# Second layer's first product in seven block products instead of eight, with block operands kept in DRAM

## The chip, the cores and the metric

The kernel runs on one core of one Trainium2 chip. The metric is device time in microseconds (us) of one execution. Engines are called PE (TensorE, the matmuls), PEld (its weight loads, which run beside it), DVE (VectorE), ACT (ScalarE), POOL (GpSimd) and SP (SyncE, which here issues the DMAs).

## The reference

An attention stage gives 2176 tokens of 512 features (4 batches of 512 tokens and 32 state rows); a first layer (512 to 1024 and back, with a softmax and a layer norm between) transforms them; a second layer follows, and it is the one that changes:

```python
def _moe2_ref(x, w_in, w_out) -> np.ndarray:      # 2176 x 512, 512 x 2048, 2048 x 512
    h = x @ w_in
    sp = np.where(h > 20.0, h, np.log1p(np.exp(np.minimum(h, 20.0))))
    g = h * np.tanh(sp)                            # the Mish function
    return (g @ w_out).astype(np.float32)
```

The weights come in as 64-bit floats and are narrowed to 32 bits in the kernel.

## The kernel before, in words

Tokens are 17 tiles of 128. Each product is computed in a split form: an operand is cut in a high part (a cast on ACT) and a low part (the subtraction of the cast, on DVE), and three matmuls stand for one, low by high, high by high and high by low. A matmul's width is the number of tokens or features that stream through it.

Phase 1 holds attention, the first layer, and what the second needs first. The order of its steps is written out in a string, PLAN, with flags that say which engine takes a step; among them `lw`, `lo`, `lx` load w_in, w_out and x; `wi` narrows w_in into w_in_t; `sp` multiplies the states by w_in_t; `a0` to `a3`, `c`, `e` run the first layer of a tile, and `d` its last product (pm, L470), whose result x goes to SBUF. `early_w2` prepares the first weights of layer 2. The program builder then sets a static order for every engine.

Phase 2 (from L559) is the second layer. The 2048 hidden features are 16 blocks f of 128. The tokens go in blocks of 3, 3, 4, 4 and 3 tiles; the first two blocks run side by side through all f, the others one after the other. `load_w2(f)` loads 512 KB of w_in and of w_out each, narrows them (`narrow`: two scalings on ACT or DVE, L45 to L50, and two DVE steps, L52 and L54), casts the high part (L134) and subtracts (L135); from then on the weights stay in SBUF. `stage_h` multiplies x by the weights of one f: twelve matmuls (four slices of 128 features, three each) of 384 or 512 columns into a bank hp of a ring of two (L590). Mish reads hp twice on ACT (L596 for the high part gh, L597 for a_), and DVE subtracts for the low part gl (L598). `stage_o`, three f behind, adds gh and gl times the output weights to po, one of six banks for each tile, three matmuls of 512 columns per tile and f (L610 to L612). For later blocks the split of x (L579, L580) is made at f = 0. A tile whose po is done is copied on ACT (L622) and stored.

## Time and profile before

| | us |
|---|---|
| three runs | 619.14, 620.29, 623.5 |
| median | 620.29 |
| profiled execution, its own time | 618.53 |
| its span, first to last instruction | 616.8 |
| PE busy in the span | 588.1 |
| DVE, ACT, POOL busy | 297.2, 266.3, 35.3 |

The profile page gives busy time per engine, a line of 40 slices of the span (tenths busy), the DMA queues, the chain of work that ended last, and the costliest groups of instructions. The trace behind it gives the start of each instruction. A busy PE is not a PE at its peak: matmuls overlap, one begins before the last has drained, so what one adds to the time is the distance from its start to the next one's.

### The profile page before, as it was taken

How to read it: one execution, taken by the hardware profiler on the slowest of the kernel's cores; microseconds unless marked ns; L12 is line 12 of the kernel's file. 1: busy time of each engine (PE TensorE's matmuls, PEld its weight loads, DVE VectorE, ACT ScalarE, POOL GpSimd, SP SyncE). 2: the span in 40 equal slices, each digit the busy share in tenths (PEclk: the TensorE clock that was granted, in tenths of full speed). 3: DMA queues.
4: the chain of work that ended last, by engine and by line, in shares of the span. 5: the costliest groups of instructions: out<-in, count | busy, mean ns of one | idle time of the engine just before them, and what ended most of it. 6: DMA issues, size and time to landing. Idle time of an engine off the chain costs nothing.

```text
span 616.8 us, 7791 instructions
## 1 busy us (share of the span) xinstructions
PE 588.1 (95%) x3048; PEld 499.5 (81%) x3048; DVE 297.2 (48%) x476; ACT 266.3 (43%) x485; POOL 35.3 (6%) x107
## 2 busy tenths in 40 slices
PE   5379999999999999999999999999999999999997
PEld 3227598779799999898998988888888888898896
DVE  3999998898578676688731121111221111211110
ACT  3786767566477652455732224221223211332211
POOL 0002131103122100000000000000000000000000
PEclk9999999999999999999999999999999999999999
DMA  8913524433445582364500002000001000011001
GB/s 346 412 42 102 156 70 123 169 103 118 172 137 175 176 223 77 137 201 137 175 1 0 1 0 104 0 1 0 1 0 70 1 0 1 0 37 33 1 1 51
DMA packets 26916, 54.77 MB, mean 89 GB/s; under 512 B 3072, under 2 KB 12800, under 8 KB 26368
## 3 DMA queue, kind: packets, MB, share of 16 engines
q1 hardware_dynamic: 26880, 54.28, 26.3%
q8 instruction: 24, 0.39, 0.3%
q14 instruction: 12, 0.10, 0.0%
HBM read 41.95 MB, written 12.32 MB: 88 GB/s over the span
## 4 chain that ended last, share of the span: by engine, by line
PE 81%; DMA 9%; DVE 5%; SPq 2%; ACT 2%; issue 1%; POOL 0%; DVEq 0%; ACTq 0%
PE hp L590 29%; PE pm L470 11%; PE po L612 10%; PE po L611 10%; PE po L610 10%; PE ph L372 6%; PE sr L301 2%; DMA wo<-in_w_out 2%; DMA w<-in_w2i 1%; DMA xT_t<-in_xT 1%; DMA wi<-in_w_in 1%; PE ph L378 1%; DMA w<-in_w2o 1%; SPq L447 1%; DMA td<-tt 1%; DVE gw_lo L354 1%
## 5 line engine op out<-in xcount | busy, mean ns | idle before, releaser
L596 ACT ACTIVATE gh<-hp 128x384 fp32r<-128x384 f32 (+1 forms) x80 | 42.6, 533 | 215.2 <-PE hp L590 206.4
L590 PE MATMUL hp<-x_lo,w2ih 128*128 128x384 f32 (+1 forms) x320 | 114.9, 359 | 1.0 <-ACT a__2378 L597 1.0
L590 PE MATMUL hp<-x_hi,w2il 128*128 128x384 f32 (+1 forms) x320 | 114.6, 359 | 0.0
L590 PE MATMUL hp<-x_hi,w2ih 128*128 128x384 f32 (+1 forms) x320 | 114.5, 358 | 0.0
L612 PE MATMUL po<-w2oh,gl 128*128 128x512 f32 x272 | 107.0, 393 | 0.0
L611 PE MATMUL po<-w2oh,gh 128*128 128x512 f32 x272 | 106.8, 393 | 0.0
L610 PE MATMUL po<-w2ol,gh 128*128 128x512 f32 x272 | 106.5, 391 | 0.0
L470 PE MATMUL pm<-ln_lo,gw_hi 128*128 128x256 f32 (+1 forms) x256 | 75.5, 296 | 0.3 <-ACT e L266 0.2
L470 PE MATMUL pm<-ln_hi,gw_hi 128*128 128x256 f32 (+1 forms) x256 | 74.5, 291 | 0.0
L470 PE MATMUL pm<-ln_hi,gw_lo 128*128 128x256 f32 (+1 forms) x256 | 74.3, 290 | 0.0
L590 PEld LDWEIGHTS hp<-x_lo,w2ih 128*128 128x128 f32 x320 | 60.1, 188 | 8.6 <-ACT a__2378 L597 1.3
L590 PEld LDWEIGHTS hp<-x_hi,w2ih 128*128 128x128 f32 x320 | 60.1, 188 | 7.3
L590 PEld LDWEIGHTS hp<-x_hi,w2il 128*128 128x128 f32 x320 | 60.1, 188 | 5.4
L612 PEld LDWEIGHTS po<-w2oh,gl 128*128 128x128 f32 x272 | 51.0, 188 | 11.3
L610 PEld LDWEIGHTS po<-w2ol,gh 128*128 128x128 f32 x272 | 51.1, 188 | 10.1 <-DVE raw_d L484 0.4
L611 PEld LDWEIGHTS po<-w2oh,gh 128*128 128x128 f32 x272 | 51.0, 188 | 9.8
L470 PEld LDWEIGHTS pm<-ln_lo,gw_hi 128*128 128x128 f32 x256 | 48.2, 189 | 1.7 <-DVE x_lo L478 0.5
L470 PEld LDWEIGHTS pm<-ln_hi,gw_hi 128*128 128x128 f32 x256 | 48.3, 189 | 0.7 <-issue 0.5
L470 PEld LDWEIGHTS pm<-ln_hi,gw_lo 128*128 128x128 f32 x256 | 48.4, 189 | 0.2
L49 ACT ACTIVATE w<-w 128x512 uint32<-128x512 uint32 x28 | 19.1, 683 | 17.4 <-DMA w<-in_w2o 8.9
L372 PE MATMUL ph<-swh,aThi 128*128 128x512 f32 x64 | 21.5, 417 | 4.5 <-DVE swl L330 4.5
L52 DVE SCALAR_TENSOR_TENSOR w<-w 128x512 uint32<-128x512 uint32 x32 | 21.9, 689 | 6.4 <-ACT w L49 6.3
(283 smaller groups left out, 755.9 us busy)
## 6 DMA issues: line engine op xcount, KB each, us to landing
w<-in_w2i SPq DMA_DIRECT2D x16, 512.0 KB, 4.1
w<-in_w2o SPq DMA_DIRECT2D x16, 512.0 KB, 3.9
td<-tt SPq DMA_DIRECT2D x13, 512.0 KB, 2.9
...
wo<-in_w_out SPq DMA_DIRECT2D x4, 1024.0 KB, 10.7
...
wi<-in_w_in SPq DMA_DIRECT2D x8, 512.0 KB, 8.0
...
```

Of the source, the lines that this page charges most:

```text
L49: nc.scalar.activation(out=low, in_=low, func=AF.Copy, scale=TOP_BITS)
L52: nc.vector.scalar_tensor_tensor(out=low, in0=high, scalar=3, in1=low, op0=ALU.logical_shift_left, op1=ALU.bitwise_or)
L301: nc.tensor.matmul(out=sr[:, j, :], lhsT=x_[:, k, :], rhs=a2[:, r0 // NS:r0 // NS + 2, k, :], start=k == 0, stop=k == 3)
L354: nc.vector.scalar_tensor_tensor(out=gw_lo[sl], in0=wr[:, k, :], scalar=g_k, in1=f32(gw_hi[sl]), op0=ALU.mult, op1=ALU.subtract)
L372: nc.tensor.matmul(out=ph[:, hf * 512:(hf + 1) * 512], lhsT=a_[:, c * P:(c + 1) * P], rhs=w_[:, q, hf * 512:(hf + 1) * 512], start=n == 0, ...
L378: nc.tensor.matmul(out=ph[:, hf * 512:(hf + 1) * 512], lhsT=xs[:, p, :], rhs=w_in_t[:, p, hf * 512:(hf + 1) * 512], start=p == 0, stop=p == 3)
L470: nc.tensor.matmul(out=pm[:, :n], lhsT=w_[:, k, m * P:(m + 1) * P], rhs=l_[:, c0:c0 + 4 * len(blk), k, :], start=cnt == 0, stop=cnt == 23)
L590: nc.tensor.matmul(out=hp[:, :n], lhsT=w_[:, k * P:(k + 1) * P], rhs=x_[:, k, x0:x0 + n], start=cnt == 0, stop=cnt == 11)
L596: nc.scalar.activation(out=gh, in_=hp[:, :n], func=AF.Mish)
L610: nc.tensor.matmul(out=po[bi, j], lhsT=gh[:, c], rhs=wl, start=f == 0, stop=False)
L611: nc.tensor.matmul(out=po[bi, j], lhsT=gh[:, c], rhs=wh, start=False, stop=False)
L612: end = nc.tensor.matmul(out=po[bi, j], lhsT=gl[:, c], rhs=wh, start=False, stop=f == NF - 1)
```

## The change

The first product of layer 2, h = x · w_in, is computed by blocks. For a pair of f's (a group, fp, eight of them) the weights are cut into four blocks (two halves of the 512 input features, two f's), the tokens of a pass into two halves, and the four block results come from seven products of sums of blocks (Winograd's form of Strassen's algorithm) rather than eight of the blocks themselves. Passes are of 6, 6 and 5 tiles, so a half has 384, 384 or 320 columns, and a product is six matmuls (`product`, L727). Of the three results that several outputs share, one is copied from PSUM by ACT (L763); seven DVE additions (L748) combine the products; Mish then reads SBUF (L757, L758).

The seven weight operands of a group, high and low, are made in pass 0 (`pieces_in`: two loads, narrowing at L46 to L55, four additions L165 to L168, five casts L175 and five subtractions L176), written to DRAM (L179), and fetched back in passes 1 and 2 (`fetch_in`, L210), into a ring of two slots. The first three groups' are made in phase 1. The seven operands of x are sums (`x_sums`, L234 to L237) and splits (`x_split`, L247 and L248); for pass 0 they are made in phase 1 after the last tiles, for a later pass in the last group of the one before. The out products (L708 to L710) are as many as before, cut in four parts that stand between the products of the next group. PLAN and its flags are new throughout.

```diff
-@N=01010011001111100 @O=0001 @P=11111111111111111 @Q=110111010011110010111001 @R=01000011 @S=11111111
-@V=00011110 @W=0001111111101100 @X=10000011 @Y=00001111111111111 @Z=00011011110110101
-lo,1,1 lb,0 lx,0 gn,1,1 sa,0 lw,1,1 ts,0 lw,2,0 fs,0,0 wi,1,1 lw,1,0 lw,3,0 te,0 tn,0 rs,0,0 lw,2,1 lw,0,1
-wi,3,0 wi,0,0 wi,1,0 fs,0,1 lw,3,1 lg sp,0,0,0,0 lo,1,0 sp,0,0,1,0 lo,0,0 tt,0,0 rs,0,1 wi,2,1 sp,0,0,0,1
...
-w,0 w,1 d,4,1 a1,15 e,10 a0,16 d,4,0 a2,14 c,13 d,5,0 a1,16 w,2 d,5,1 a2,16 a3,14 e,13 e,12 a2,15 a3,15 c,15
-d,6,1 a3,16 c,16 c,14 e,15 w,4 e,14 d,6,0 e,16 d,7,1 d,7,0 w,3
...
+a3,4 a1,6 c,3 a1,7 s2,0 lx,3 e,2 c,4 e,4 a3,5 a0,9 a0,8 a1,9 a2,6 a2,7 a3,6 a3,7 c,6 c,5 ln,2 e,3 a1,8
...
-    def load_w2(f, pool):
-        for nm, src in (("i", w2i[f]), ("o", w2o[f])):
-            hi = pool.tile([P, 512], F32R, name=f"w2{nm}h{f}")
-            lo = pool.tile([P, 512], F32R, name=f"w2{nm}l{f}")
-            w64 = w64_p.tile([P, 512, 2], U32, tag="w64", name="w64")
-            nc.sync.dma_start(out=w64, in_=src)
-            w = f32(w64[..., 0])
-            narrow(nc, w, w64, eng('W', f, False, True), how(12 + f))
+
+
+    A11, A12, A22, S1, S2, S3, S4 = range(7)
+    B11, B21, B22, T1, T2, T3, T4 = range(7)
...
+    def ring(fp):
+
+        if fp % 2 == 0:
+            return [[(0, 7, sw_o.tile([P, 7, 256], F32R, tag=t, name="w2" + t))] for t in ("swh", "swl")]
+        t = x2p.tile([P, 2, 6, 256], F32R, tag="x1", name="w2r")
+        r = wx_p.tile([P, 2, 1, 256], F32R, tag="wx1", name="w2r1")
...
+    def pieces_in(fp, stage=False):
+
+        w = []
+        for j in range(2):
...
+        s1, s2, s3, s4 = ea[:, :256], ea[:, 256:], eb[:, :256], eb[:, 256:]
+        on = eng('G', fp, nc.vector, nc.gpsimd)
+        on.tensor_tensor(out=s1, in0=a21, in1=a22, op=ALU.add)
+        on.tensor_tensor(out=s3, in0=a11, in1=a21, op=ALU.subtract)
...
+        for i, n, src in ((A11, 1, a11), (A12, 1, a12), (A22, 1, a22), (S1, 2, ea), (S3, 2, eb)):
+            if i in (A11, S1):
+                yield
+            src = src.rearrange("p (n c) -> p n c", c=256)
+            hi, lo = (operands(place, i, n) for place in places)
...
+            nc.vector.tensor_tensor(out=lo, in0=src, in1=f32(hi), op=ALU.subtract)
+        for place, d in zip(places, kept[fp]):
+            for i, n, w in place:
+                nc.sync.dma_start(out=d[:, i:i + n], in_=f32(w))
+        if stage:
+            staged.add(fp)
+        else:
+            W["i", fp] = places
...
+    def pieces_out(fp, pool=None):
+        for j in range(2):
+            f = 2 * fp + j
+            if pool is None:
...
+            w, _ = load64(w2o[f], 1, f)
+            yield
...
-            eng('L', f, nc.gpsimd, nc.vector).tensor_tensor(out=lo, in0=w, in1=f32(hi), op=ALU.subtract)
-            W[nm, f] = (hi, lo)
+            eng('H', fp, nc.vector, nc.gpsimd).tensor_tensor(out=lo, in0=w, in1=f32(hi), op=ALU.subtract)
...
+    def fetch_in(fp):
+        W["i", fp] = ring(fp)
+        for place, d in zip(W["i", fp], kept[fp]):
+            for i, n, w in place:
+                nc.sync.dma_start(out=f32(w), in_=d[:, i:i + n])
...
+
+    HALVES = [([("a", 0, 384)], [("a", 384, 384)]),
+              ([("c", 0, 256), ("d", 0, 128)], [("c", 256, 256), ("d", 128, 128)]),
+              ([("d", 256, 320)], [("d", 576, 320)])]
+    xop = {}
...
+    def x_sums(ps):
+
+        t = x2p.tile([P, 4, 2, 384], F32, tag="x1" if ps == 0 else "x0", name="xsum")
+        for o, n, b11, b21, b12, b22 in halves(ps):
+            t1, t2, t3, t4 = (t[:, i, :, o:o + n] for i in range(4))
+            nc.vector.tensor_tensor(out=t1, in0=b12, in1=b11, op=ALU.subtract)
+            nc.vector.tensor_tensor(out=t2, in0=b22, in1=t1, op=ALU.subtract)
+            nc.vector.tensor_tensor(out=t3, in0=b22, in1=b12, op=ALU.subtract)
+            nc.vector.tensor_tensor(out=t4, in0=b21, in1=t2, op=ALU.subtract)
...
+    def x_split(ps, i):
+        x = tl["E"].tile([P, 2, 2, 384], F32R, tag=f"xo{i}", name=f"xo{i}")
+        for o, n, b11, b21, b12, b22 in halves(ps):
...
+            nc.scalar.copy(out=hi, in_=src)
+            nc.vector.tensor_tensor(out=lo, in0=src, in1=f32(hi), op=ALU.subtract)
+        xop[i] = (x[:, 0], x[:, 1])
...
-                if d0 < 6:
-                    o = slice(d0 * P, d0 * P + n)
-                    nc.scalar.copy(out=x_hi[:, m, o], in_=pm[:, :n])
-                    nc.vector.tensor_tensor(out=x_lo[:, m, o], in0=pm[:, :n], in1=f32(x_hi[:, m, o]), op=ALU.subtract)
-                elif d0 < 10:
-                    o0 = (d0 - 6) * P
-                    copy(out=raw_c[:, m, o0:o0 + n], in_=pm[:, :n])
-                else:
-                    o0 = (d0 - 10) * P
-                    copy(out=last_view()[:, m, o0:o0 + n], in_=pm[:, :n])
+                o0 = (d0 - base) * P
+                copy(out=raw[t][:, m, o0:o0 + n], in_=pm[:, :n])
...
-        def stage_h(bi, f, n):
...
-            if bi == 0 and f >= NE:
-                load_w2(f, w2p)
-            hp = ps_g.tile([P, 512], F32, tag="hp", name="hp")
-            wh, wl = W["i", f]
-            cnt = 0
-            for k in range(4):
-                for w_, x_ in ((wh, x_lo), (wh, x_hi), (wl, x_hi)):
-                    nc.tensor.matmul(out=hp[:, :n], lhsT=w_[:, k * P:(k + 1) * P], rhs=x_[:, k, x0:x0 + n],
-                                     start=cnt == 0, stop=cnt == 11)
...
-            gs[bi, f] = (gh, gl)
-
         po = {}
...
-        seq = [(bi, f) for f in range(NF) for bi in range(2)] + [(bi, f) for bi in range(2, 5) for f in range(NF)]
-        for i in range(len(seq) + LAG - 2):
-            if i < len(seq):
-                bi, f = seq[i]
-                stage_h(bi, f, sizes[bi] * P)
...
+        def out_parts(ps, fp):
+
+            n, nh = tiles[ps], tiles[ps] // 2
+            f0, f1 = 2 * fp, 2 * fp + 1
+            if fp < NFP - 1:
+                low, high = range(nh), range(nh, n)
+                parts = [[(f0, j) for j in low], [(f1, j) for j in low],
+                         [(f1, j) for j in high], [(f0, j) for j in high]]
...
+                m = -(-len(steps) // 4)
...
+            def product(*terms):
+                r = bank()
+                cnt = 0
+                for a, x in terms:
+                    wh, wl = (operands(place, a) for place in W["i", fp])
+                    for k in range(2):
+                        for w_, x_ in ((wh, x[1]), (wh, x[0]), (wl, x[0])):
+                            nc.tensor.matmul(out=r, lhsT=w_[:, 0, k * P:(k + 1) * P], rhs=x_[:, k, :n],
+                                             start=cnt == 0, stop=cnt == 6 * len(terms) - 1)
+                            cnt += 1
+                return r
+
+            def step(a, b):
...
+                if last:
+                    x_split(ps + 1, b)
+                for _ in range(1 if b in (B11, T3) else 2):
+                    next(more, None)
+                return r
...
+            def bank():
+                return ps_g.tile([P, 512], F32, tag="hp", name="hp")[:, :n]
...
+            part = iter(parts)
+            m1_ = temp("m1")
+            nc.scalar.copy(out=m1_, in_=step(A11, B11))
+            active(add("c0", m1_, step(A12, B21)), 0, 0)
+            next(part)()
+            u2 = add("u2", m1_, step(S2, T2))
+            u3 = add("u3", u2, step(S3, T3))
+            next(part)()
+            active(add("c1", u3, step(A22, T4)), 1, 0)
+            m5 = step(S1, T1)
+            active(add("c2", u3, m5), 1, 1)
+            u4 = add("m1", u2, m5)
+            next(part)()
+            active(add("c0", u4, step(S4, B22)), 0, 1)
+            next(part)()
...
+        for ps in range(NPASS):
+            for fp in range(NFP):
+                ahead = fp + 1
+                more = iter(())
+                if ps == 0 and 2 <= ahead < NFP:
+                    more = pieces_out(ahead, w2p)
+                    if ahead in staged:
+                        fetch_in(ahead)
+                    else:
+                        more = chain(pieces_in(ahead), more)
+                elif ps > 0 and ahead < NFP:
+                    fetch_in(ahead)
+                if ps + 1 < NPASS and fp == NFP - 1:
+                    fetch_in(0)
+                if ps + 1 < NPASS and fp == NFP - 2:
+                    x_sums(ps + 1)
+                group(ps, fp, parts, more)
+                for _ in more:
```

On PE, in the middle of phase 2 of before, one run of `stage_h` and the out products ahead of it read (name, operation, operands, width; a wait names the engine that must have got that far; DMAHW5 and the like are DMA queues):

```order
L611 MATMUL po<-w2oh_3204,gh 128x512
L612 MATMUL po<-w2oh_3204,gl 128x512
L590 MATMUL hp<-x_lo,w2ih_3346 128x384 [waits Activation_49]
L590 MATMUL hp<-x_hi,w2ih_3346 128x384
L590 MATMUL hp<-x_hi,w2il_3347 128x384
L590 MATMUL hp<-x_lo,w2ih_3346 128x384
L590 MATMUL hp<-x_hi,w2ih_3346 128x384
L590 MATMUL hp<-x_hi,w2il_3347 128x384
L590 MATMUL hp<-x_lo,w2ih_3346 128x384
L590 MATMUL hp<-x_hi,w2ih_3346 128x384
```

After, in the second pass, out products lead to the fifth, sixth and seventh product of a group (xo_3595, xo_3613, xo_3642 are three of the operands of x, w2swh and w2swl the ring's weights):

```order
L727 MATMUL hp<-xo_3595,w2swl 128x384
L727 MATMUL hp<-xo_3613,w2swh 128x384 [waits DVE_49]
L727 MATMUL hp<-xo_3613,w2swh 128x384
L727 MATMUL hp<-xo_3613,w2swl 128x384
L727 MATMUL hp<-xo_3613,w2swh 128x384 x2
L727 MATMUL hp<-xo_3613,w2swl 128x384
L727 MATMUL hp<-xo_3642,w2swh 128x384 [waits DVE_49]
L727 MATMUL hp<-xo_3642,w2swh 128x384
L727 MATMUL hp<-xo_3642,w2swl 128x384
L727 MATMUL hp<-xo_3642,w2swh 128x384 x2
L727 MATMUL hp<-xo_3642,w2swl 128x384
L708 MATMUL po<-w2ol_2516,gh 128x512 [waits Activation_49]
```

Where one run of twelve waited once, for ACT, three runs of six now follow each other, each with a wait for DVE, without out products between them.

On DVE, in the stretch in which layer 2's weights are prepared, before (w_2816 and so on are loaded weights, w2il and w2ol low parts):

```order
L54 SCALAR_TENSOR_TENSOR w_2816<-w_2816 128x512 [waits DVE_49]
L598 TENSOR_TENSOR gl<-a__2515,gh 128x384 [waits PE_49,Activation_49]
L135 TENSOR_TENSOR w2il_2815<-w_2816,w2ih_2814 128x512 [waits Activation_49]
L45 TENSOR_SCALAR w_2826<-w_2826 128x512 [waits DMAHW5_49]
L52 SCALAR_TENSOR_TENSOR w_2826<-w_2826 128x512 [waits DVE_49,Activation_49]
L45 TENSOR_SCALAR w_2892<-w_2892 128x512 [waits DMAHW6_49]
L54 SCALAR_TENSOR_TENSOR w_2826<-w_2826 128x512 [waits DVE_49]
L52 SCALAR_TENSOR_TENSOR w_2892<-w_2892 128x512 [waits DVE_49,Activation_49]
L598 TENSOR_TENSOR gl<-a__2543,gh 128x384 [waits PE_49,Activation_49]
L45 TENSOR_SCALAR w_2902<-w_2902 128x512 [waits DMAHW7_49]
L54 SCALAR_TENSOR_TENSOR w_2892<-w_2892 128x512 [waits DVE_49]
L135 TENSOR_TENSOR w2ol_2825<-w_2826,w2oh_2824 128x512 [waits Activation_49]
```

After, in a group of pass 0 (c, u and m are the results of the additions of hp):

```order
L53 SCALAR_TENSOR_TENSOR w_2831<-w_2831 128x512 [waits DMAHW0_49,Activation_49]
L55 SCALAR_TENSOR_TENSOR w_2831<-w_2831 128x512 [waits DVE_49]
L748 TENSOR_TENSOR u_2733<-hp,u_2714 128x384 [waits PE_49]
L165 TENSOR_TENSOR w_2817<-w_2831 128x256 [waits DVE_49]
L166 TENSOR_TENSOR w_2831<-w_2817,w_2831 128x256
L167 TENSOR_TENSOR w_2817<-w_2817 128x256 [waits DVE_49]
L168 TENSOR_TENSOR w_2831<-w_2817 128x256 [waits DVE_49]
L53 SCALAR_TENSOR_TENSOR w_2879<-w_2879 128x512 [waits DMAHW2_49,Activation_49]
L748 TENSOR_TENSOR c_2753<-hp,u_2733 128x384 [waits PE_49]
L55 SCALAR_TENSOR_TENSOR w_2879<-w_2879 128x512 [waits DVE_49]
L748 TENSOR_TENSOR c_2766<-hp,u_2733 128x384 [waits PE_49]
L748 TENSOR_TENSOR m_2772<-hp,u_2714 128x384
```

Between the narrowing steps of the loaded weights there now stand the additions that read hp and wait for PE, and those of the weights among each other; two narrowing steps in a row wait one for the other.

On SP, which issues the DMAs in order, before, in the same stretch:

```order
L131 DMA w_2664<-in_w2i 128x1024 [waits DMAHW5_49,DVE_49]
L131 DMA w_2674<-in_w2o 128x1024 [waits DMAHW6_49,DMAHW1_49,DVE_49]
L131 DMA w_2740<-in_w2i 128x1024 [waits DMAHW7_49,DMAHW2_49,DVE_49]
L131 DMA w_2750<-in_w2o 128x1024 [waits DMAHW3_49,DMAHW0_49,DVE_49]
L131 DMA w_2816<-in_w2i 128x1024 [waits DMAHW4_49,DMAHW1_49,DVE_49]
L131 DMA w_2826<-in_w2o 128x1024 [waits DMAHW2_49,DVE_49]
```

After (k4h and k4l are the DRAM copies of a group's operands):

```order
L151 DMA w_2898<-in_w2o 128x1024 [waits DMAHW3_49,DMAHW2_49,DVE_49]
L179 DMA k4h<-w2swh 128x1792 [waits DMAHW4_49,Activation_49]
L151 DMA w_2988<-in_w2i 128x1024 [waits DMAHW6_49,DVE_49]
L179 DMA k4l<-w2swl 128x1792 [waits DVE_49]
L151 DMA w_3002<-in_w2i 128x1024 [waits DMAHW7_49,DMAHW0_49]
L151 DMA w_3052<-in_w2o 128x1024 [waits DMAHW3_49,DVE_49]
L179 DMA k5h<-w2r_3013 128x256 [waits DMAHW1_49,Activation_49]
L179 DMA k5l<-w2r_3013 128x256 [waits DVE_49]
L151 DMA w_3071<-in_w2o 128x1024 [waits DMAHW0_49,DVE_49]
```

The loads alternated, each behind the load three before it; now the stores of one group's operands, which wait for the last cast and the last subtraction, stand ahead of the next group's loads.

## Rows read from the trace of the kernel before

**Rows 1.** The page, busy us, share of the span, and count by engine.

```profile
PE 588.1 (95%) x3048; PEld 499.5 (81%) x3048; DVE 297.2 (48%) x476; ACT 266.3 (43%) x485; POOL 35.3 (6%) x107
```

**Rows 2.** Waits of PE: what for, us in total, times, longest.

```profile
PE ph L323 <- DVE w_in_t L54: 10.3, 1, 10.3
PE ph L199 <- DMA xT_t<-in_xT: 7.2, 1, 7.2
PE ph L372 <- DVE swl L330: 4.5, 2, 3.7
```

**Rows 3.** Stretches: length, busy PE, PEld, DVE, ACT, POOL, granted clock, DMA share, GB/s.

```profile
40.00:60.00 20.00, 15.21 (x78) 11.76 (x79) 19.44 (x38) 11.86 (x26) 2.51 (x9) 0.91 0.22 67
...
100.00:250.00 150.00, 148.62 (x957) 133.07 (x957) 115.01 (x168) 86.87 (x148) 20.66 (x56) 1.00 0.47 146
...
250.00:265.00 15.00, 15.00 (x75) 13.16 (x74) 12.14 (x23) 8.54 (x16) 0.00 (x0) 1.00 0.54 181
```

**Rows 4.** The page: the chain that ended last, share by line.

```profile
PE hp L590 29%; PE pm L470 11%; PE po L612 10%; PE po L611 10%; PE po L610 10%; PE ph L372 6%; PE sr L301 2%; DMA wo<-in_w_out 2%; DMA w<-in_w2i 1%; DMA xT_t<-in_xT 1%; DMA wi<-in_w_in 1%; PE ph L378 1%; DMA w<-in_w2o 1%; SPq L447 1%; DMA td<-tt 1%; DVE gw_lo L354 1%
```

**Rows 5.** The chain in order of time: start, us, what, count of instructions.

```profile
140.85 2.94 PE pm L470 x24
...
256.34 2.09 PE hp L590 x12
...
516.42 2.72 PE hp L590 x12
```

**Rows 6.** Instructions by line and form: count, busy us, mean ns, idle before.

```profile
L590 PE MATMUL hp<-x_lo,w2ih 128*128 128x384 f32 x192 | 64.7, 337 | 1.0 <-ACT a__2378 L597 1.0
...
L590 PEld LDWEIGHTS hp<-x_lo,w2ih 128*128 128x128 f32 x320 | 60.1, 188 | 8.6 <-ACT a__2378 L597 1.3 <-ACT a__2799 L597 0.2
...
L590 PE MATMUL hp<-x_lo,w2ih 128*128 128x512 f32 x128 | 50.2, 392 | 0.0
```

**Rows 7.** DVE instructions in order: start, duration, line, operation, shape.

```profile
222.12 0.69 DVE L52 SCALAR_TENSOR_TENSOR w<-w 128x512 uint32<-128x512 uint32 x1
222.84 0.69 DVE L54 SCALAR_TENSOR_TENSOR w<-w 128x512 uint32<-128x512 uint32 x1
...
226.10 0.69 DVE L135 TENSOR_TENSOR w2il<-w,w2ih 128x512 fp32r<-128x512 f32 x1
226.70 0.42 DVE L484 COPY raw_d<-pm 128x256 f32<-128x256 f32 x1
227.04 0.68 DVE L135 TENSOR_TENSOR w2ol<-w,w2oh 128x512 fp32r<-128x512 f32 x1
...
255.81 0.55 DVE L598 TENSOR_TENSOR gl<-a__2459,gh 128x384 fp32r<-128x384 f32 x1
256.27 0.42 DVE L45 TENSOR_SCALAR w<-w 128x512 f32<-128x512 f32 x1
```

**Rows 8.** ACT instructions in order, same columns.

```profile
260.48 0.70 ACT L49 ACTIVATE w<-w 128x512 uint32<-128x512 uint32 x1 [0.32 <-DMA w<-in_w2i]
261.07 0.67 ACT L134 CAST w2oh<-w 128x512 fp32r<-128x512 f32 x1
261.71 0.49 ACT L596 ACTIVATE gh<-hp 128x384 fp32r<-128x384 f32 x1
262.10 0.49 ACT L597 ACTIVATE a__2515<-hp 128x384 f32<-128x384 f32 x1
```

**Rows 9.** The page: GB/s in 40 slices, the mean, and transfers (KB, median us to landing).

```profile
GB/s 346 412 42 102 156 70 123 169 103 118 172 137 175 176 223 77 137 201 137 175 1 0 1 0 104 0 1 0 1 0 70 1 0 1 0 37 33 1 1 51
DMA packets 26916, 54.77 MB, mean 89 GB/s; under 512 B 3072, under 2 KB 12800, under 8 KB 26368
...
w<-in_w2i SPq DMA_DIRECT2D x16, 512.0 KB, 4.1
...
wo<-in_w_out SPq DMA_DIRECT2D x4, 1024.0 KB, 10.7
...
wi<-in_w_in SPq DMA_DIRECT2D x8, 512.0 KB, 8.0
```

231 lines of the change are left out of this document (140 added, 91 removed).

## The prediction, made before the changed kernel ran

> **What bounds the kernel now.** I read the shares first: TensorE (PE) is busy 95% of the span, DVE 48%, ACT 43% [rows 1]. A share is an average over stages, so I went to what PE waits for: some 25 us in all, in three large pieces (w_in_t, xT_t, swl), and all three products that wait stand in the opening [rows 2]. The second layer's own product hp waits 1.0 us in the whole run [rows 6]. The table of stretches says the same: between 40 and 60 us PE is busy 15.2 of 20 us and DVE 19.4; between 100 and 250 us PE is busy 148.6 of 150, at a granted clock of 1.00, the upper of its two levels, and DVE 115 [rows 3]. So from about 70 us the time is the sum of the matmuls' pitches, and the chain that ended last agrees: hp alone is 29% of it, pm and po another 41% [rows 4]. A kernel like that gets faster only by fewer or narrower matmuls, as long as the work that replaces them hides on DVE, ACT and the DMA queue. The reader should therefore see two things: what a matmul costs by its width, and how much of each other engine is free in each stage.
>
> **What it removes.** The pitch (from start to start, which is what adds up on PE) comes from the chain: twelve hp matmuls 384 wide take 2.09 us, 174.5 ns each; twelve 512 wide 2.72 us, 227 ns; twenty-four pm matmuls 256 wide 2.94 us, 122.5 ns [rows 5]. Busy durations (337 and 392 ns, [rows 6]) overlap and don't add. Before, hp is 48 runs of twelve at 384 and 32 at 512 (192 and 128 of each of three kinds, [rows 6]): 48 x 2.095 + 32 x 2.72 = 187.6 us. After: 24 groups (a pair of f's in a pass) of seven products of six matmuls, 672 of them 384 wide and 336 of them 320 wide. No row has 320. Bounds: at the price of 256 it is 122.5 ns, at that of 384 174.5. Halfway in columns is halfway in price between them (148.5), and 512 lies on the same line (174.5 + 52 = 226.5), so I take 148.5. Sum 672 x 0.1745 + 336 x 0.1485 = 167.2 us. Gain 20.4 us, between 11.7 (320 at the price of 384) and 29.2 (at that of 256). The weight loads (188 ns each, [rows 6]) don't set these pitches: pm has the same loads and a pitch of 122.5.
>
> The out products keep their 816 matmuls of 512: nothing.
>
> The Trainium skill puts an isolated back-to-back matmul at N/2.4 + 2.5 ns ("TensorE: Matmul & The Clock Gate", Back-to-back issue gap), 162.5 ns at 384, 216 at 512 and 136 at 320; by it the gain would be estimated at 21.6 us. The rows are 11 to 12 ns above it at 384 and 512, so the sum keeps the rows' prices.
>
> **What it adds in a group of the last two passes.** PE needs 7 x 1.05 + 36 out matmuls (8.3) = 15.6 us per group, 5/6 of it, 13.2, in the pass of five tiles. DVE gets seven adds and four gl subtractions 384 wide. A subtraction of that width starts the next 0.45 us later [rows 7]: 11 x 0.46 = 5.1 us. ACT gets eight Mish at 0.39 and one copy [rows 8]: 3.5 us. Both hide under 15.6 us. Fetching the operands is 2 x 0.917 MB per group. The nearest stretch with steady loads moved 181 GB/s at a DMA share of 0.54, and two slices of the opening moved 346 and 412 [rows 3, 9]: 1.83 MB takes 10.1 us at the first and 5 at the second, in 13.2 to 15.6. Hidden, since a slot of the ring is free a whole group ahead.
>
> The one tight place is in the order: the fifth, sixth and seventh product run back to back on two banks, and the seventh needs the bank of the fifth, which the add c1 reads. Between them lies the sixth, 1.05 us. The fifth's last matmul drains 0.17 us into it (0.34 long at a pitch of 0.17, [rows 6]), and c1 is 0.55 long [rows 7]: 0.33 us remain for two hand-overs on an idle DVE, some 0.25 at 320, so I take no stall in passes 1 and 2. If DVE is still in a 0.60 us piece, the seventh product waits some 0.35 us.
>
> **What it adds in pass 0.** There the operands are made. Five groups carry a full preparation (f pairs 3 to 7): DVE has eight narrowing steps of 512 at 0.60 to 0.72, two and five subtractions (four of 0.60, three of 0.34), four adds of 256 (0.34), and the 5.1 us from above [rows 7]: 5.0 + 2.4 + 1.0 + 1.35 + 5.1 = 14.9 us of 15.6. ACT: eight narrowings and two casts of 512 at 0.59, five casts 2.1, Mish and copy 3.5 [rows 8]: 11.5. DMA: 2.1 MB in, 1.83 MB out, 3.9 MB in 15.6 us or 250 GB/s, above the 181 of today's loading stretch and below the 346 of the opening. In today's loading stretch DVE is busy 12.1 of 15 us and PE never waits [rows 3]. Now DVE is at 95% by starts, and SP sends the load of a pair behind the store of the pair before it, whose wait is for that pair's last cast; so loading, narrowing, adds, casts and subtractions of one pair are a loop of nearly one group. A load landed within 4.1 us at the median [rows 9]. What is late next: the first product of the next group, then its adds. Bounds: nothing (14.9 < 15.6), and 2.9 us a group if DVE gets only 80% of the time for these steps, as in today's stretch (14.9 / 0.8 = 18.6), 15 us over five. I take 0.8 us a group, nearer to nothing because PE's static order leaves each add but c1 two us of out matmuls as cover: **+4 us**.
>
> **What it adds in phase 1.** DVE gets the sums of x for two passes, 7.2 us (four of 768, at 0.87 on the line through 0.46 for 384 and 0.60 for 512, [rows 7], and four of 512 with four of 256), seven splits of 768, 6.1, and three preparations' adds, 4.1, less twelve x_lo of 256, 4.0: +13.4 us. DVE is idle 35 us between 100 and 250 us [rows 3], where these stand, so most is covered; the splits come last, before the first product. I put the wait at the seam at +2 us (0 if all is covered, 6.1 if all seven splits are bare). The plan of the opening is a new one: a 1 MB wo load and three preparations of w_in ahead of xT, where PE waits for w_in_t for 10.3 us and for xT_t 7.2 today. DVE is full there (19.4 of 20 us), and steps in other order shift by one or two loads: I take +1.5 us, between -3 and +5 (one wo landed in a median 10.7 us, a w_in half in 8.0, [rows 9]). Tile 10 is now turned by eight more PE transposes and one part goes through DRAM instead: +0.5 us.
>
> **Sum.** 618.5 (the profiled execution) - 20.4 + 4 + 2 + 1.5 + 0.5 = 606.1. That execution is 1.8 us under the median of the three runs shown (619.1 to 623.5), so **608 us** against 620.3.
>
> **The rivals.**
> *All hidden.* If DVE at 95% suffices and the seam is covered: 618.5 - 20.4 + 0.5 + 1.8 = 600 us. For it: PE does not wait for hp today beyond 1.0 us. Against: DVE has 0.7 us to spare per group. 2 in 10.
> *Pass 0 becomes the bound.* DVE and the queue make 18.6 us a group: 608 - 4 + 15 = 619, no change to be seen. For it: the loop above, with two waits on SP in it, and narrowing pairs that depend on each other go at 0.72 rather than 0.60. Against: five groups only. Anything from 613 to 620; 2 in 10.
> *The fetch is not hidden* (ends on the other side). In 16 groups PE would wait for 1.83 MB. It decides below 1.83 MB / 15.6 us = 117 GB/s (139 in the short pass); each us that it is late costs 16 us. The kernel gets slower by over 1% at about 1.2 us late per group, 109 GB/s; at the mean of today's span, 89 GB/s [rows 9], it would be 20.6 us a group, 5 late, some 690 us. Against: the mean of the span includes idle stretches; the loading stretches moved 181. Half in 10.
> *The clock.* With two banks and seven hand-overs a group, PE might stop often enough to be granted the lower level, as in the one stretch where it waits today (0.91 between 40 and 60 us, [rows 3]). Ten us at half speed cost 5 us: about 613. Under half in 10.
> The Trainium skill names this pattern, cycling through PSUM banks with small idle times between groups so that the clock swings ("TensorE: Matmul & The Clock Gate", A second HAM failure mode: psum-queue depth-cycling). Today's hp also cycles through two banks at 1.00, so the trace doesn't bear it out so far.
>
> **How the numbers follow.** The forecast itself (pass 0 loses 1 to 8 us, seam and opening 1 or 2 us to either side: 603 to 612) has 5 in 10. The range takes in the clean case from below and most of the saturated one: 599 to 618. One per cent, 6.2 us, is about what a measurement of this kernel tells from no change. Faster by more (under 614.1): the forecast, the clean case and the nearest part of the saturated and clock cases, 0.78; within it 0.17; slower 0.05.
>
> **What would show it.** Twelve-fold hp runs become six-fold, 1.05 us at 384 and near 0.89 at 320; groups in passes 1 and 2 start 15.6 and 13.2 us apart with PE busy throughout. Waits of PE for the first product's operands, or for c1, should stand in pass 0 alone, with DVE near full there and under half full later. If groups of passes 1 and 2 are further apart, the fetch or c1 is wrong; if 320 is paced like 384, 8.7 us of the gain go; if the first hp product starts more than 5 us later than today's, phase 1 is.

## The result, and the profile after

The kernel after took 615.23 us (median of eleven runs, 613.38 to 617.51), the kernel before 621.05 in the same comparison: a ratio of 0.9904, 95% interval 0.9879 to 0.9929. It is faster, by just under 1%; the time lies within the range, but 5.8 us went, where 12 were forecast. One run of the kernel before, at 664.88 us, was slow and is not in the ratio; without it the median of the others is 620.67.

The page's first part, and its slices of DVE and of the granted clock (40 slices of 15.3 us):

```profile
PE 574.9 (94%) x3108; PEld 500.6 (82%) x3108; DVE 411.9 (67%) x729; ACT 309.9 (51%) x592; POOL 32.3 (5%) x105
...
DVE  4799989989899866778889797333333463343332
...
PEclk9977999999999997999999999999999999999999
```

The clock line of before:

```profile
PEclk9999999999999999999999999999999999999999
```

Against [rows 1] PE is busy 13 us less and DVE 115 us more. From slice 3 to slice 25, the end of pass 0, DVE is between 60% and over 90% busy, and about a third after that. The clock line has dips that before doesn't have, in slices 3 and 4 (the opening) and in slice 16.

PE's waits (in [rows 2] they were three large pieces in the opening):

```profile
PE ph L315 <- DMA xT_t<-in_xT: 11.3, 1, 11.3
PE pm L584 <- DVE ln_lo L565: 5.1, 1, 5.1
PE ph L439 <- DVE w_in_t L55: 4.0, 2, 2.6
PE tr L405 <- DVE aTlo L345: 3.6, 1, 3.6
PE tr L340 <- DVE ex L334: 2.3, 1, 2.3
PE hp L727 <- ACT w2swh L175: 1.8, 1, 1.8
...
PE hp L727 <- DVE c L748: 1.0, 2, 0.6
```

The second and the sixth line are new in kind: they stand between phase 1 and phase 2. The wait of a product for an addition (the last line), which the forecast feared in pass 0, is 1.0 us in the whole run. The stretches (columns as in [rows 3]) say where and for how long:

```profile
200.00:220.00 20.00, 19.80 (x155) 19.15 (x153) 15.56 (x22) 11.06 (x18) 2.42 (x8) 1.00 0.52 156
220.00:240.00 20.00, 12.71 (x61) 11.99 (x62) 12.63 (x22) 9.74 (x19) 0.00 (x0) 0.83 0.78 270
240.00:260.00 20.00, 18.80 (x104) 17.91 (x103) 15.06 (x30) 11.02 (x19) 0.00 (x0) 1.00 0.56 203
...
360.00:380.00 20.00, 20.00 (x101) 18.11 (x101) 17.62 (x35) 14.93 (x34) 0.00 (x0) 1.00 0.79 287
...
400.00:500.00 100.00, 100.00 (x502) 90.76 (x501) 41.55 (x77) 31.84 (x65) 0.00 (x0) 1.00 0.31 112
```

Between 220 and 240 us, at the seam of phases 1 and 2, PE stands for 7.3 of 20 us; from there to 400 us it stands for 2.2, and in pass 1 not at all. The chain in order of time shows the later groups:

```profile
416.73 3.18 PE hp L727 x18
...
432.38 3.18 PE hp L727 x18
...
535.55 2.64 PE hp L727 x18
...
548.65 2.63 PE hp L727 x18
```

The three products in a row take 3.18 us, 176.7 ns a matmul, against 174.5 in [rows 5]; at 320 columns 2.635 us, 146.4 ns, against the forecast's 148.5. Groups start 15.65 and 13.10 us apart, as forecast (15.6, 13.2).

To put numbers on it I priced every matmul of a trace: the median distance from start to start of its product and shape (in the trace of after; the 512-wide hp from before), times its count, is PE's own work; the time that has passed less the work done up to there is what PE has lost, in waits and at the lower clock. The last column ends with PE's last matmul.

| us | PE's own work | lost to 100 us | 100 to 220 | 220 to 260 | 260 to 400 | from 400 |
|---|---|---|---|---|---|---|
| before | 575.6 | 29.2 | 5.8 | 1.5 | 0.8 | 0.1 |
| after | 555.9 | 30.9 | 7.4 | 12.7 | 1.7 | 0.7 |
| after less before | -19.7 | +1.7 | +1.6 | **+11.2** | +0.9 | +0.6 |
| forecast | -19.9 | +1.5 | 0 | +2 | +4 | 0 |

The work went as forecast, to 0.2 us (by this account of two profiled executions). More than half of the gain was lost again in 40 us at the seam.

### The profile page after: what moved, and what is told of

The parts are those of the page before. It is cut to its first block, busy times and chain, and to the rows that moved or that the text cites. A ratio compares the mean times of both kernels' runs of the same rounds, so it can differ in the third digit from the quotient of the medians.

```text
span 613.4 us, 8430 instructions
## 1 busy us (share of the span) xinstructions
PE 574.9 (94%) x3108; PEld 500.6 (82%) x3108; DVE 411.9 (67%) x729; ACT 309.9 (51%) x592; POOL 32.3 (5%) x105
## 4 chain that ended last, share of the span: by engine, by line
PE 70%; DMA 10%; DVE 10%; ACT 4%; SPq 2%; issue 2%; POOL 0%; ACTq 0%; DVEq 0%
PE hp L727 23%; PE pm L584 9%; PE po L708 9%; PE po L709 9%; PE po L710 9%; PE ph L488 5%; DMA w<-in_w2o 2%; DMA w<-in_w2i 2%; DMA ln_lo<-td 2%; PE sr L417 1%; SPq L563 1%; DMA td<-tt 1%; DMA xT_t<-in_xT 1%; PE ph L315 1%; DVE tt L550 1%
## 5 line engine op out<-in xcount | busy, mean ns | idle before, releaser
L757 ACT ACTIVATE gh<-c 128x384 fp32r<-128x384 f32 (+1 forms) x96 | 48.7, 507 | 148.4 <-DVE c L748 147.1
L708 PE MATMUL po<-w2ol,gh 128*128 128x512 f32 x272 | 106.8, 393 | 0.8 <-ACT gh L757 0.8
L727 PE MATMUL hp<-xo,w2r 128*128 128x384 f32 (+1 forms) x504 | 93.8, 329 | 0.6 <-DVE c L748 0.6
L727 PEld LDWEIGHTS hp<-xo,w2r 128*128 128x128 f32 x504 | 86.4, 188 | 5.7 <-DVE c L748 1.0
L727 PE MATMUL hp<-xo,w2swh 128*128 128x384 f32 (+1 forms) x336 | 82.8, 330 | 2.6 <-ACT w2swh L175 1.8
L710 PE MATMUL po<-w2oh,gl 128*128 128x512 f32 x272 | 82.5, 392 | 0.0
L727 PEld LDWEIGHTS hp<-xo,w2swh 128*128 128x128 f32 x336 | 60.6, 188 | 8.3 <-ACT w2swh L175 2.0
L708 PEld LDWEIGHTS po<-w2ol,gh 128*128 128x128 f32 x272 | 51.1, 188 | 10.1 <-ACT gh L757 1.6
L710 PEld LDWEIGHTS po<-w2oh,gl 128*128 128x128 f32 x272 | 50.1, 188 | 7.5
L727 PE MATMUL hp<-xo,w2swl 128*128 128x384 f32 (+1 forms) x168 | 55.1, 329 | 0.0
L748 DVE TENSOR_TENSOR c<-hp,u 128x384 f32<-128x384 f32 (+1 forms) x48 | 25.5, 533 | 42.2 <-PE hp L727 42.2
L748 DVE TENSOR_TENSOR c<-hp,m 128x384 f32<-128x384 f32 (+1 forms) x48 | 25.4, 530 | 38.4 <-PE hp L727 37.3
L727 PEld LDWEIGHTS hp<-xo,w2swl 128*128 128x128 f32 x168 | 31.5, 188 | 0.2 <-DVE w2swl L176 0.2
```

Of the source, the lines that this page charges most:

```text
L708: nc.tensor.matmul(out=po[ps, j], lhsT=gh[:, c], rhs=wl, start=first, stop=False)
L710: nc.tensor.matmul(out=po[ps, j], lhsT=gl[:, c], rhs=wh, start=False, stop=f == NF - 1)
L727: nc.tensor.matmul(out=r, lhsT=w_[:, 0, k * P:(k + 1) * P], rhs=x_[:, k, :n], start=cnt == 0, stop=cnt == 6 * len(terms) - 1)
L748: nc.vector.tensor_tensor(out=r, in0=y, in1=x, op=ALU.add)
L757: nc.scalar.activation(out=gh, in_=src, func=AF.Mish)
```

## What was tried on the chip

Each run was profiled and timed beside the kernel before; a ratio is to that. "Lost" is meant as in the table. An edit can also change the static order, since the program builder makes it anew; where that matters it is said. The losses are those of one profiled execution, which can lie some 3 us from the median: 617.55 against 620.80 with the loads held behind, 633.49 against 630.50 in the run without the cover.

### What happens at the seam

These are the rows of PE in the kernel after, in order of start; a bracket gives the idle time ahead and what ended it:

```profile
220.38 0.39 PE L584 MATMUL pm<-ln_lo,gw_hi 128*128 128x256 f32 x1 [0.58 <-ACT raw_d L590]
...
225.38 0.96 PE L727 MATMUL hp<-xo,w2swh 128*128 128x384 f32 x4 [1.84 <-ACT w2swh L175]
...
232.92 0.69 PE L584 MATMUL pm<-ln_lo,gw_hi 128*128 128x384 f32 x1 [5.07 <-DVE ln_lo L565]
233.41 0.52 PE L584 MATMUL pm<-ln_hi,gw_hi 128*128 128x384 f32 x1
233.72 0.52 PE L584 MATMUL pm<-ln_hi,gw_lo 128*128 128x384 f32 x1
```

The last block of layer 1's product (three tiles, 384 wide) waits for the low part of the last tile, 16, until 232.92. In the 9.7 us since the last matmul of the block before it started, PE has twelve hp matmuls to do, two products, 2.1 us. After the wait its matmuls start 0.32 us apart rather than 0.18; the windows put the granted clock of 230 to 235 at 0.70 and of 235 to 240 at 0.62, so PE is at the lower of its two levels for a while: by the chain the block's first 72 matmuls take 15.69 us, where 72 x 0.178 would be 12.8, which costs another 2.9. The tile's way: transposed ("turned") on DVE at 214.7, stored to DRAM (td), brought back by four DMAs (ln_lo), cast, subtracted. The store took 8.0 us to land, where 3.0 is the median; two 512 KB loads of layer 2's weights are issued just ahead of it.

**Theory A**: the seam is lost to that way through DRAM, late because of the weights' loads. **Theory B**: DVE's new work ahead of the last tiles' layer norm sets the seam. Against both: the preparation does it, or PE was not the bound at all.

### Tile 16 turned by PE

```diff
-@Y=00001111110111111
+@Y=00001111110111110
```

> One flag is changed: the last tile (16) is turned by eight PE transposes instead of through DRAM. Theory A (the seam is lost to the way of tile 16 through DRAM: its store waited 8.0 us behind two weight loads, its four loads stand behind it and behind the product before, and PE waits 5.1 us for ln_lo, after which the clock is at its lower level for some 5 us): the wait for ln_lo falls under 2 us, the granted clock between 220 and 250 us stays near 1.00, and 5 to 8 us of the 615.2 go, to 607 to 610; PE pays 1 us for the transposes. Theory B (DVE's additions for the second layer stand ahead of the last tiles' layer norm and set the seam): the wait moves to another reader of DVE, and 0 to 2 us go.

Measured: 613.02 us (609.32 to 614.01), ratio 0.9863 (0.9830 to 0.9896). The two stretches, of this kernel:

```profile
220.00:260.00 40.00, 36.69 (x205) 35.09 (x206) 29.58 (x55) 22.80 (x42) 0.00 (x0) 0.96 0.64 229
260.00:400.00 140.00, 136.64 (x678) 122.24 (x677) 105.41 (x210) 79.39 (x165) 0.00 (x0) 1.00 0.53 190
```

Lost between 220 and 260 us: 5.7 in place of 12.7, and the clock stays higher. So the way of the last tile is what PE waits for; the rest of Theory A's forecast came short: 2.6 us of the wait for ln_lo are left, and 2 us went rather than 5 to 8. But between 260 and 400 it now loses 4.7 in place of 1.7: pass 0 takes back 3 of the 7 us. While PE stood at the seam the preparation had run ahead; with less of a stop, products wait for additions (3.4 us, five waits, against 1.0 in two), as the forecast had it for pass 0.

### The weights' loads behind tile 16

```diff
-            w.append(load64(w2i[2 * fp + j], 0, 2 * fp + j))
+            with after(*([last_turn[0]] if fp == 0 else [])):
+                w.append(load64(w2i[2 * fp + j], 0, 2 * fp + j))
```

(and in PLAN `d,6,0 e,16` ahead of `pi,0`; `last_turn` is the DMA that brings the tile back.)

> The loads of the first group's weights are issued behind the four loads that bring tile 16 back from DRAM; nothing else is changed but what the static order makes of it. If it is the weight loads in front that made the store of tile 16 late (8.0 us instead of 3), its landing falls to 3 to 4 us, PE's wait for ln_lo comes down by 2 to 3 us, but the first products of layer 2 come later, for want of weights: 612 to 617 in all. If the loads in front don't matter, the wait for ln_lo is as long as before and the time 617 to 621, since layer 2 begins later.

Measured: 620.80 us, ratio 1.0007 (0.9982 to 1.0031). The tile's store now lands in 2.9 us rather than 8.0, and the last ln_lo is done at 229.12 rather than 232.86. At the seam 9.6 us are lost in place of 12.7, so the loads in front did cost some 3; but PE stands 6.4 us in one piece, since the first products now come after the last block and cover nothing. The time is the one forecast for the case that the loads don't matter, though they did: what was gained on the tile was lost on the products. Pass 0 loses 7.0, having started its preparation later. The loads in front are not the main cause.

### Sums held back

```diff
-                    x_sums(ps + 1)
+                    with after(held[0]):
+                        x_sums(ps + 1)
```

(`held` is the last addition of the group before.)

> The sums of x for passes 1 and 2 (7.2 us of DVE, of which 3.7 stood between 199 and 213 us, in the middle of the last tiles' layer norm) are held back until an addition of the sixth group of the pass before. Theory B (DVE at the seam): last tiles' ln_lo comes 3 to 4 us earlier, 610 to 612. Theory A (DMA way of tile 16): the wait for ln_lo changes by less than 1.5 us and the time by as much, 614 to 616, except where the order of DMAs changes with it.

Measured: 617.15 us, ratio 0.9935 (0.9918 to 0.9951). DVE is busy 11.6 of 20 us between 200 and 220 in place of 15.6, and PE's wait for ln_lo falls from 5.1 to 1.7; the waits that end last are now these:

```profile
PE hp L727 <- ACT w2swh L175: 4.8, 1, 4.8
PE hp L727 <- ACT m L763: 1.9, 1, 1.9
PE pm L584 <- DVE ln_lo L565: 1.7, 1, 1.7
```

At the seam 12.6 us are lost, where it was 12.7. The order of SP changed with the edit, too: the weights' loads now stand behind the store of the last tile. PE's shorter wait does not mean an earlier tile: its low part is done at 235.35, 2.5 us later than without the edit, and PE stands for the first product's weights first. Theory B finds no support, since freeing DVE gave nothing, but with the changed order the run is no clean test of it.

### Seven products less one

```diff
-            active(add("c0", u4, step(S4, B22)), 0, 1)
+            active(add("c0", u4, u2), 0, 1)
```

> Left out: the seventh product of every group (its addition takes another operand that is there). If phase 2 is bound by PE throughout, each of the 24 products gives back its pitch, 16 x 1.055 + 8 x 0.885 = 24 us: 591. If DVE or the DMA queue bounds pass 0, its eight groups give back nothing, and 15.5 us go: 600. If the fetch bounds the last two passes, 8.4 us go: 607.

Measured: 596.02 us, ratio 0.9600 (0.9581 to 0.9619), 19 us under the kernel after. PE's work fell by 23.8; of that pass 0 took back 3.8 (5.5 lost in place of 1.7) and the later passes 1.2. Phase 2 is bound by PE; the term that the forecast rests on is sound.

### Fetching twice

```diff
-                nc.sync.dma_start(out=f32(w), in_=d[:, i:i + n])
+                for _ in range(2):
+                    nc.sync.dma_start(out=f32(w), in_=d[:, i:i + n])
```

> The kernel after, with each fetch of operands from DRAM made twice, one after the other, to the same place. If the fetch is hidden with much room (1.83 MB in 15.6 us), 3.7 MB per group, 235 GB/s and 280 in the last pass, still fits: 614 to 617. If the fetch stood near its limit, groups of passes 1 and 2 move apart by 2 to 5 us: 650 to 690.

Measured: 626.60 us, ratio 1.0088 (1.0054 to 1.0122). In the middle of pass 1 nothing is lost:

```profile
400.00:500.00 100.00, 100.00 (x500) 90.53 (x499) 37.36 (x70) 28.12 (x59) 0.00 (x0) 1.00 0.68 246
```

246 GB/s where the kernel after moved 112, and PE still busy throughout. The 11 us go in pass 0 (10.3 lost in place of 1.7, 5.1 of them between 280 and 300 us, where group 2's operands are needed, fetched among the loads and stores) and 2.4 later, in the short groups. So neither outcome of the expectation came. The rival of a fetch that is not hidden falls for pass 1, where there is room to double it; in pass 0 there is none.

### Stores on other queues; subtractions on GpSimd

These stand on the run with tile 16 turned by PE, to find what makes pass 0 lose 4.7 us.

```diff
-                nc.sync.dma_start(out=d[:, i:i + n], in_=f32(w))
+                nc.gpsimd.dma_start(out=d[:, i:i + n], in_=f32(w))
```

> Stands on the run with tile 16 turned by PE (613.0 us), where the seam gave back 7 us and pass 0 then lost 4.7 (the kernel after lost 0.8 in the same stretch). The stores of the operands to DRAM are issued from GpSimd's queue rather than from SP's. Theory C (in pass 0 the loads of the next pair stand on SP behind stores that wait for the last cast, 22 us of waits there, so that they land late and DVE's additions queue behind narrowing steps that wait for them): loads start earlier, PE's 3.4 us of waits for additions between 280 and 370 fall under 1.5, and the time comes to 608 to 611. Theory D (DVE has no time left in pass 0, loads or not): the waits stay, 612 to 615. If only bandwidth counts (stores and loads share it): no change either, with landings of 5 to 9 us as before.

> As the run with stores on GpSimd's queue, but from ACT's. ACT then stands still until the subtraction behind a low store is done, so Mish comes later: worse than on GpSimd by 1 to 5 us if ACT matters in pass 0, and the same 608 to 611 if it does not.

Measured: 621.11 us from GpSimd's queue (ratio 0.9999, 0.9975 to 1.0023), 619.53 from ACT's (0.9978, 0.9955 to 1.0001). Pass 0 lost 10.4 and 6.6 us, and 608 to 611 came from neither. SP's waits between 260 and 400 us, with the stores on SP and then with the stores on GpSimd:

```profile
SPq L179 <- ACT w2r L175: 22.3, 6, 6.6
SPq L151 <- DVE w2ol L195: 20.2, 4, 8.4
```

```profile
SPq L151 <- DVE w2ol L195: 37.4, 7, 8.5
SPq L151 <- DVE w2r L176: 26.4, 4, 8.8
```

Theory C's forecast fails: without stores ahead of them the loads wait for their buffers instead, which DVE's last step on the pair before frees. Why pass 0 lost more than with the stores on SP is not shown; the order is new in both runs.

The subtractions of the output weights on GpSimd (`@H=11111111`):

> Also on the run with tile 16 turned by PE. The two subtractions per pair of the output weights go from DVE to GpSimd, 1.2 us per group less on DVE in pass 0. Theory D (DVE's time): the waits between 280 and 370 us fall by half or more, 609 to 611. Theory C (late loads): they stay, 612 to 614, or grow, since a slower subtraction holds the loaded buffer longer, up to 617.

Measured: 618.93 us, ratio 0.9960 (0.9936 to 0.9984). Pass 0 lost 5.6 us with 1.2 us less for DVE in each group, so Theory D found no support; the opening and the seam came out worse too (41.7 us lost to 220, 9.5 at the seam), with a new order.

### Preparation left out

On the run with tile 16 turned by PE; all groups from 3 on fetch group 2's operands:

```diff
-                    if ahead in staged:
-                        fetch_in(ahead)
-                    else:
-                        more = chain(pieces_in(ahead), more)
+                    fetch_in(ahead)
...
-        for place, d in zip(W["i", fp], kept[fp]):
+        for place, d in zip(W["i", fp], kept[min(fp, 2)]):
```

> On the run with tile 16 turned by PE (613.0 us). Left out: the making of the input-weight operands of groups 3 to 7 in pass 0 (loads, narrowing, additions, casts, subtractions, stores); those groups use group 2's operands, fetched from DRAM as in the later passes. The output weights are still prepared. Theory E (pass 0 is bound by the preparation as a whole, which takes back what the seam gives): the 4.7 us that PE lost between 260 and 400 us fall under 1, 608 to 609.5. Theory F (the additions of the products themselves are late, preparation or not): they stay, 612 to 614.

Measured: 610.51 us, ratio 0.9829 (0.9798 to 0.9860). The stretch that holds the groups without preparation:

```profile
260.00:300.00 40.00, 37.79 (x186) 33.34 (x186) 32.51 (x58) 26.95 (x52) 0.00 (x0) 1.00 0.66 243
300.00:400.00 100.00, 100.00 (x501) 90.58 (x500) 45.46 (x87) 34.40 (x74) 0.00 (x0) 1.00 0.35 127
```

From 300 us on PE never waits; with the preparation it had lost 3.3 in that stretch. Theory F falls: the additions of the products are no burden by themselves. Theory E is borne out there, but not whole, since 3.1 us are lost ahead of 300, more than the 1 it allowed. Most of that is one wait of 2.2 us for an addition at 290.89, in a group without preparation of input weights; ahead of that addition DVE had stood for 1.3 us for a load of output weights and then worked on them. Their preparation was left in. In time the run can't be told from the one with tile 16 alone (0.9863, 0.9830 to 0.9896).

> As the run before it, and the operands of groups 0 and 1 are not made either but fetched from group 2's, so that the seam is free of preparation too. If preparation at the seam and in pass 0 is all that stands between the kernel and the saving of PE's own work (18 us), what is left of the lag is the opening's: 601 to 605. If the seam is lost to the last tiles' layer norm, preparation or not, it stays above 607.

Measured: 613.85 us, ratio 0.9890 (0.9852 to 0.9929). Pass 0 loses 0.6 us, but the seam 8.3, with DVE busy 18.2 of 40 us there:

```profile
PE pm L583 <- DVE ln_lo L545: 4.5, 1, 4.5
```

The wait for the last tiles is there with no preparation of input weights at the seam at all. That left the question why the kernel before doesn't have it.

### The cover

In the kernel before, the last three tiles go the same way through DRAM. But between 203 and 232 us its PE does this, where layer 1's product pauses (the first matmul of each run of 24; after the third run layer 1's last block begins):

```profile
203.52 0.34 PE L590 MATMUL hp<-x_lo,w2ih 128*128 128x384 f32 x1
...
222.09 0.34 PE L590 MATMUL hp<-x_lo,w2ih 128*128 128x384 f32 x1
...
227.40 0.44 PE L590 MATMUL hp<-x_lo,w2ih 128*128 128x384 f32 x1 [0.96 <-ACT a__2378 L597]
...
231.67 0.34 PE L470 MATMUL pm<-ln_lo,gw_hi 128*128 128x384 f32 x1
```

72 matmuls of layer 2, 12.5 us of work, fill the gaps. The last tile comes little earlier there; this is the step that ends its low part, before and after:

```profile
229.31 1.22 DVE L449 TENSOR_TENSOR ln_lo<-ln_lo,ln_hi 128x1024 fp32r<-128x1024 f32 x1
231.64 1.23 DVE L565 TENSOR_TENSOR ln_lo<-ln_lo,ln_hi 128x1024 fp32r<-128x1024 f32 x1
```

It is done at 230.53 and at 232.86, so of the 11.2 us more that are lost at the seam at most 2.3 are a later tile (not counting its share in the clock's part). With the loads held behind it was done at 229.12, earlier than in the kernel before, and 9.6 us were lost. **Theory G**: the kernel after lost that cover. To try it, the cover was taken from the kernel before:

```diff
-                    nc.tensor.matmul(out=hp[:, :n], lhsT=w_[:, k * P:(k + 1) * P], rhs=x_[:, k, x0:x0 + n],
+                    with after(*([tl["last"]] if cnt == 0 and (bi, f) == (0, 0) else [])):
+                        nc.tensor.matmul(out=hp[:, :n], lhsT=w_[:, k * P:(k + 1) * P], rhs=x_[:, k, x0:x0 + n],
```

(`tl["last"]` is the last matmul of layer 1's last product.)

> The kernel before, with one change: layer 2's first product may not start until the last matmul of layer 1's last product is issued. In the kernel before, 72 matmuls of layer 2 (12.5 us) stand in three gaps between 203 and 232 us, while the last tiles' layer norm is on its way; in the kernel after only 12 (2.1 us) do. Theory G (the seam's loss is the lost cover: PE has nothing else to do while the last tiles come): PE then waits 7 to 11 us at the seam, as the kernel after does, and the time is 627 to 632. Theory A alone (the way through DRAM is late only in the kernel after, because of the weights' loads): the wait stays under 4 us, 620 to 624.

Measured: 630.50 us, ratio 1.0154 (1.0100 to 1.0208). PE's waits between 195 and 400 us, and the stretch at the seam:

```profile
PE pm L470 <- DVE ln_lo L449: 9.2, 1, 9.2
PE pm L470 <- ACT raw_d L484: 1.7, 1, 1.7
```

```profile
220.00:240.00 20.00, 10.82 (x63) 10.61 (x62) 15.09 (x27) 7.23 (x10) 0.00 (x0) 0.74 0.65 188
```

The kernel before now has the seam of the kernel after: 10.8 us lost between 220 and 260 (1.5 without the edit), 9.2 in one wait for ln_lo, and the clock down; 3.4 more are lost between 100 and 220, where the first of the gaps lies. (The profiled execution also lost 2.1 more in the opening, which the edit doesn't touch.) The work did not change, and by the medians (630.50 against 619.93) the cover was worth 10.6 us. Theory G stands.

Why only two products fit ahead in the kernel after shows in ACT's first copy of a product:

```profile
252.72 0.48 ACT L763 COPY m<-hp 128x384 f32<-128x384 f32 x1 [2.44 <-PE pm L584]
```

The first product was done before 228, but its copy waits until layer 1's last matmul. I took the reason to be that the buffer m1 lies where that matmul's operands lie; the next run bears it out. With two banks of hp full, PE can't start a third product. So the buffers of the combined products were put in a pool ahead of the other, where the layer norm's inputs had been:

```diff
+        wt = ph2.enter_context(tc.tile_pool(name="wt", bufs=1, reuse_waits="tile"))
         wk = ph2.enter_context(tc.tile_pool(name="wk", bufs=1, reuse_waits="tile"))
...
-                return wk.tile([P, 384], F32, tag=name, name=name)[:, :n]
+                return wt.tile([P, 384], F32, tag=name, name=name)[:, :n]
```

> The kernel after, with the buffers of the combined products (m1, c0, u2, u3, c1, c2) in a pool of their own, laid where the layer norm's inputs were, in place of one laid over what the last product of layer 1 reads. In the kernel after, the copy of the first product waited for that last product (ACT's wait at 252.7 us), so that only two products fit ahead of it. Theory G: three products stand ahead of it, 1 to 3 us of the seam go, 612 to 614.5, unless pass 0 takes them back. If cover is not what the seam lacks: 615 as before.

Measured: 613.81 us, ratio 0.9900 (0.9866 to 0.9933); the kernel after had 0.9904, so the time can't be told from it. But the copy now starts at 228.71, and at the seam 6.4 us are lost in place of 12.7, with 23 hp matmuls ahead of the last of layer 1 in place of 12, and no wait for ln_lo (2.7 us of waits for the first weights are left); pass 0 lost 3.4 in place of 1.7, and the profiled opening 3.7 more than that of after, which the edit does not explain.

> Both: tile 16 turned by PE and the buffers moved, nothing left out. Theory G with theory E (pass 0's preparation takes back part of what the seam gives): 609 to 613, against 613.0 with tile 16 alone. If they don't add up: 613 to 616.

Measured: 612.35 us (611.24 to 612.91), ratio 0.9851 (0.9804 to 0.9898). Lost at the seam 4.5 us, in pass 0 5.4. It is the best median of all that leave nothing out, with tile 16 alone (0.9863) within its interval. The gains at the seam overlap (8.2 us together, 7.0 and 6.3 alone), and pass 0 takes 3.7 of them back. The whole cover of 72 matmuls was given back in no run, so what it would bring the kernel after in time is not shown.

### Two more tries

Tile 16 by PE with the sums held back:

> A try at a faster kernel with nothing left out: tile 16 turned by PE and the sums of x for the later passes held back until the sixth group of the pass before. At the seam that frees 3.7 us of DVE where the first kernel still lost 5.7 us (2.6 of them for ln_lo); in pass 0 it adds 3.7 us to DVE in one group. If the seam is DVE's, 2 to 3 us go, 610 to 611; if pass 0 takes back what the seam gives, as it did with tile 16, 612 to 615.

Measured: 616.10 us, ratio 0.9914 (0.9880 to 0.9949); 8.0 us lost at the seam in place of 5.7, so none of the 2 to 3 gained, and 2.7 in pass 0; both forecasts were missed, with a new order and more lost up to 220 us, too.

On the run with both edits (612.35), a load buffer of its own for the output weights in pass 0:

```diff
-        w64 = w64_p.tile([P, 512, 2], U32, tag="w64", name="w64")
+        own = i == 1 and "w64o" in tl
+        w64 = (tl["w64o"] if own else w64_p).tile([P, 512, 2], U32, tag="w64", name="w64")
```

> The run with tile 16 turned by PE and the products' buffers moved (612.4 us), plus one buffer of 4 KB per partition, used in pass 0 alone for the loads of the output weights, which until now share three buffers with those of the input weights. With the stores moved to another queue, SP's loads waited for those buffers instead (37 us for the one that holds output weights). Theory H (the three buffers hold pass 0's preparation back): the 5.4 us that PE still loses between 260 and 400 us fall to 2 or less, 608 to 610. If the loop is held by DVE's order and its waits on PE and ACT, whenever the loads land: 611 to 614.

Measured: 622.16 us, ratio 1.0022 (0.9992 to 1.0052). Pass 0 lost 13.8 us, more than ever, with another order. Theory H finds no support. What in the preparation holds pass 0 (the order of DVE, the landing of loads, or the waits between ACT and DVE) is not settled by these runs; that it is the preparation, is: with that of the input weights left out, 0.6 us were lost.

## Why the prediction was wrong, by its own steps

**What bounds the kernel** was read rightly but for the seam: after the opening the time is PE's own work. Leaving out a product per group gave 19 of 24 us.

**What it removes**: 20.4 us less 0.5, forecast -19.9; -19.7 measured. The price at 320 columns was 146.4 ns against 148.5, that of 384 in a product of six 176.7 against 174.5; the two errors, -0.7 and +1.5 us, cancel in part. The rows' prices were the better ones. The Trainium skill's formula for an isolated matmul ("TensorE: Matmul & The Clock Gate", Back-to-back issue gap) would give 162.5 at 384 columns and 136 at 320, both below what was measured.

**The last two passes**: right, in pitch of the groups, in the additions that hide, and in the tight place at the seventh product, which costs next to nothing (PE busy 100 of 100 us, 0.7 us lost from 400 us on).

**Pass 0**: +4 forecast, +0.9 measured. That it came out small looks like luck: PE stood at the seam while the preparation ran ahead, and the runs that lost less at the seam lost 4.7, 3.4 and 5.4 us in pass 0, near the forecast's size. The two terms were added as if they were independent; in these runs the later one takes back part of what the earlier one saves.

**The seam**: this step failed. The forecast put +2 us there, because DVE had 35 us free between 100 and 250 us. That is an account of DVE's time; PE's time at the seam hung on something else, on what PE had to do while the last tiles were on their way. In before those were layer 2's own first products, and the change took them away, since the new products need more buffers than two banks, some of which lie on memory that layer 1 still reads (the first copy waited to 252.72, and to 228.71 once they were moved), and weights that have to be made first (1.8 us of wait). Measured: +11.2 us, nearly twice the 6.1 that the forecast had as its worst case, of which 2.9 are the lower clock after the wait and at most 2.3 a later tile. Its own sign of being wrong came, too: the first hp product starts at 225.38, 21.9 us later than in the kernel before (203.52). The forecast's own question, what hides this and what does it cost if the cover is gone, was asked of the new work and not of the old.

**The opening**: +1.5 forecast, +1.7 measured to 100 us, and 1.6 more up to 220.

**The offset**: 1.8 us were added because the profiled execution of before lay under the median. Over eleven runs that was 2.5, and the profiled execution of after lies on its median; so the spans differ by 3.4 us (the table's columns add up to 3.7) and the medians by 5.8.

**The rivals**: "all hidden" did not come. "Pass 0 becomes the bound" was wrong in place, though 615 lies in its 613 to 620, by luck. "The fetch is not hidden" was far from it: twice the fetch fits in pass 1. "The clock" came in part, not from hand-overs in phase 2, where from 240 us on it is 1.00 with seven hand-overs a group, but behind the long wait at the seam, and in the opening (0.91 and 0.66 in the two stretches of 20 us from 20 to 60, against 1.00 and 0.91 before), where the loss grew by 1.7 us in all. The cycling through banks of which the Trainium skill warns ("TensorE: Matmul & The Clock Gate", A second HAM failure mode: psum-queue depth-cycling) is not borne out by this 1.00 in phase 2.
